# A GEGLU feed-forward kernel: two half loads of w_gate move from SyncE's DMA queue to ScalarE's

## The chip, the core and the metric

The kernel runs on one core of a Trainium2 chip. A core has TensorE (PE: matmuls, with the weight loads, PEld, beside them), VectorE (DVE), ScalarE (ACT), GpSimd (POOL) and SyncE (SP). Sixteen DMA engines move data between the chip's memory (HBM) and the core's on-chip memory (SBUF). A DMA is started by an instruction in the stream of some engine; in this kernel only SP and ACT do so. In the trace, `SPq` and `ACTq` mark those issuing instructions, and `q1` and `q10` are the two hardware queues that SP's and ACT's transfers travel on. Each engine works through its own instruction stream in order, so an issue that takes long holds up what stands behind it in that stream.

The metric is device time in microseconds (us) of one execution. The kernel before takes 276.43 us (median of 3 runs, 276.41 to 276.88).

## The reference

```python
def reference(x, w_gate, w_up, w_down):
    return (_gelu(x @ w_gate) * (x @ w_up)) @ w_down
```

`x` is 32 x 32 x 1024, that is 1024 rows of D = 1024; `w_gate` and `w_up` are 1024 x 3584 (F = 3584), `w_down` is 3584 x 1024. All are bf16; `_gelu` is the tanh approximation.

## The kernel before, in words

Stage 1 computes, for each of the 28 blocks of 128 columns of F, the gate and the up product against both halves of the rows (512 each), applies Gelu, multiplies, and keeps the result in `gT`. It saves matmuls with a seven-product scheme of the Strassen kind on 2 x 2 blocks: the inner dimension is split in two halves of KH = 4 tiles of 128, the weights' blocks are `a11`, `a12` (gate, first and second half of D) and `a21`, `a22` (up), and the blocks of x are `B11`, `B21` (first 512 rows, in the tile `xt0`) and `B12`, `B22` (last 512 rows, in `xt1`). Stage 2 multiplies `gT` by `w_down`, again with seven products.

A w_gate tile (`WG[c]`, line 86 loads it) holds two blocks of F; its first half in D serves `first_products` (a11 x B11), its second half `second_products` (a12 x B21). So `WG[1]` serves blocks 2 and 3, and `WG[4]` blocks 8 and 9. x comes in by three transposing DMAs on SP: B11 (line 131), B21 (line 149), and xt1 (line 155), which is twice as large.

The order of the work is written out by hand, and the streams keep it. At the start:

- PE runs ten warming matmuls (line 137), then `first_products` for blocks 0 to 7, `second_products` for blocks 0 to 7, first 8 and 9, second 8 and 9, first 10 (which needs `WG[5]`'s first half), and then the products on sums of x: T1 x S1, first 11, and T2 x S2.
- ACT issues six loads (WG0 in three pieces, the first halves of WG1, WG2 and WG3) between the warming matmuls, then copies each first product out of PSUM into `E1` (line 213), turns each second product into Gelu (line 220), seeds two accumulators `X` (line 226) after the Gelus of blocks 5 and 6, and copies the first products of blocks 8 and 9. A block's second product accumulates onto its first product in the same PSUM bank, so `second_products(n)` starts only when ACT's copy of block n is done.
- SP issues B11, then, after a small ACT write into B21 (line 147) that holds it back, B21, then the second halves of WG1 and WG2, half of the first w_up tile (line 93), the second half of WG3, the whole of WG4, xt1, both halves of WG5, and the other half of the w_up tile.
- DVE makes the sums of weights for blocks 0 and 1 and then the sums T1 to T4 of x, for which it needs xt1.

Of the kernel before, what the change touches and what calls it, by code (L numbers as in the profile page):

```python
# [12 lines left out]
def kernel(  # L13
# [18 lines left out]
    nc = tc.nc  # L32
# [10 lines left out]
    DT = D // P  # L43
    KH = DT // 2
# [38 lines left out]
    def load_gate(c, queue, lo=0, hi=DT):  # L83
        if c not in WG:
            WG[c] = gw.tile([P, DT, 2 * P], bf16, name="gw", tag="gw")
        queue.dma_start(  # L86
            out=WG[c][:, lo:hi, :], in_=wg_r[:, lo:hi, 2 * c * P : (2 * c + 2) * P]
        )

    def load_up(c, lo=0, hi=4):  # L90
        if c not in WU:
            WU[c] = uw.tile([P, DT, 4 * P], bf16, name="uw", tag="uw")
        nc.sync.dma_start(  # L93
            out=WU[c][:, :, lo * P : hi * P],
            in_=wu_r[:, :, (4 * c + lo) * P : (4 * c + hi) * P],
        )
# [4 lines left out]
    def a11(i):  # L101
        return block(WG, 2, i, 0)

    def a12(i):
        return block(WG, 2, i, 1)
# [18 lines left out]
    def psum_p(name):  # L124
        return psum.tile([P, NB], fp32, name=name, tag="p")

    def psum_q(name):
        return psum.tile([P, NB], fp32, name=name, tag="q")

    with tc.manual_schedule():  # L130
# [16 lines left out]
                nc.scalar.activation(B21[:, 0, 0:8], table, ACT.Copy)  # L147
                nc.scalar.activation(table, ones[:, 0:8], ACT.Gelu_apprx_tanh)
        nc.sync.dma_start_transpose(out=B21, in_=xf[0:NB, KH * P : D])
        for c in (1, 2):  # L150
            load_gate(c, nc.sync, KH, DT)
        load_up(0, 0, 2)
        load_gate(3, nc.sync, KH, DT)
        load_gate(4, nc.sync)
        nc.sync.dma_start_transpose(out=xt1, in_=xf[NB:N, :])  # L155
        load_gate(5, nc.sync, 0, KH)
        load_gate(5, nc.sync, KH, DT)
# [6 lines left out]
        def t_sum(name, a, b, step=2):  # L164
            for k in range(0, KH, step):
                ks = slice(k, k + step)
                nc.vector.tensor_tensor(T[name][:, ks, :], a[:, ks, :], b[:, ks, :], ALU.subtract)
# [24 lines left out]
        def pair_product(ps, lhs, rhs, first, cuts):  # L192
            for lo, hi in zip(cuts, cuts[1:]):
                for p, l in zip(ps, lhs):
                    for k in range(lo, hi):
                        nc.tensor.matmul(  # L196
                            p,
                            lhsT=l[:, k, :],
                            rhs=rhs[:, k, :],
                            start=(first and k == 0),  # L200
                            stop=(k == KH - 1),
                            skip_group_check=True,
                        )

        def first_products(*blocks, cuts=(0, KH)):
            for i in blocks:
                A[i] = psum_p("a") if 4 <= i < 8 else psum_q("a")
            pair_product([A[i] for i in blocks], [a11(i) for i in blocks], B11, True, cuts)
            for i in blocks:
                if i % 2 == 0:  # L210
                    pool, tag = (xpool, "e1") if i == LEAD - 2 else (ring, "ring")
                    E1[i // 2] = pool.tile([P, 2, NB], fp32, name="e1", tag=tag)
                nc.scalar.activation(E1[i // 2][:, i % 2, :], A[i], ACT.Copy)  # L213

        def second_products(*blocks, cuts=(0, KH)):
            pair_product([A[i] for i in blocks], [a12(i) for i in blocks], B21, False, cuts)
            for i in blocks:
                if i % 2 == 0:
                    GL[i // 2] = half.tile([P, 2, NB], bf16, name="gl0", tag="half")
                nc.scalar.activation(GL[i // 2][:, i % 2, :], A[i], ACT.Gelu_apprx_tanh)  # L220
# [3 lines left out]
        def seed(i):  # L224
            X[i] = psum_p("x")
            nc.scalar.activation(X[i], E1[i // 2][:, i % 2, :], ACT.Copy)
# [51 lines left out]
        t_sum("T3", B22, B12)  # L278
        t_sum("T4", B21, T["T2"])
        first_products(0, 1, cuts=(0, 2, KH))  # L280
        for n in range(2, 8):
            first_products(n)
        for n in range(8):
            second_products(n)
            if n in (5, 6):
                seed(n - 5)
        first_products(8)
# [34 lines left out]
        for i in range(2, FT + 1):  # L322
# [24 lines left out]
            if here and i % 2 == 0:  # L347
                c = i // 2 + (6 if i < 8 else 4)
# [194 lines left out]
```

## Time and profile before

| what | value |
|---|---|
| median of 3 runs | 276.43 us (276.41 to 276.88) |
| the profiled execution's own time | 276.04 us |
| its span, first to last instruction | 274.2 us |
| PE busy | 269.2 us, 98% of the span |
| ACT busy | 139.6 us, 51% |
| DVE busy | 189.2 us, 69% |
| POOL busy | 87.1 us, 32% |
| granted PE clock | 1.000 |
| read from HBM | 22.02 MB |

The span leaves out 1.8 us of the profiled execution that lie around it, and the profiled execution is 0.39 us below the median. An issue's row (`SPq`, `ACTq`) gives the time the issuing engine spent on the instruction, not the transfer; the time to landing is listed apart, per group. "Waits" rows tell how long an engine stood idle before an instruction and what released it. The chain of waits follows the work that ended last backwards from the end; printed in order of time it shows what set the time of each stretch.

### The profile page before, as it was taken

The numbers are of one execution on the slowest core, as the hardware profiler recorded it, in microseconds if no ns is written. First come the engines' busy times: TensorE is split into PE (matmuls) and PEld (weight loads), VectorE is DVE, ScalarE is ACT, GpSimd is POOL, SyncE is SP. The second block draws the span as 40 slices with busy tenths as digits, with TensorE's granted clock in tenths as the row PEclk, the third lists the DMA queues.
The fourth block names the chain that finished last, engine by engine and source line by source line (L and its number), as shares of the span: only waits on it lengthen the run. The fifth ranks groups of instructions, "written<-read, shape, count | busy, mean of one in ns | idle before, by whom it ended". The sixth has DMA issues, their size and how long they took to land.

```text
span 274.2 us, 3352 instructions
## 1 busy us (share of the span) xinstructions
PE 269.2 (98%) x1186; PEld 189.5 (69%) x1186; DVE 189.2 (69%) x226; ACT 139.6 (51%) x240; POOL 87.1 (32%) x81
## 2 busy tenths in 40 slices
PE   8998999999999999999999999999999999999995
PEld 2444677768777687776877768764447888888883
DVE  0068985866668666686666766759994999999800
ACT  4787765566556665566665666531100072770311
POOL 0000075845558455584455844600000000000000
PEclk9999999999999999999999999999999999999999
DMA  7999402153400034216370202359702000000221
GB/s 190 271 257 272 160 1 76 44 188 101 129 2 0 0 95 138 76 36 195 91 217 0 76 2 77 112 189 318 226 0 77 2 0 0 1 2 0 97 96 38
DMA packets 41024, 26.42 MB, mean 96 GB/s; under 512 B 9264, under 2 KB 41008, under 8 KB 41008
## 3 DMA queue, kind: packets, MB, share of 16 engines
q1 hardware_dynamic: 38208, 24.78, 30.7%
q10 hardware_dynamic: 2800, 1.44, 2.1%
q8 instruction: 9, 0.15, 0.2%
q14 instruction: 7, 0.06, 0.1%
HBM read 22.02 MB, written 2.10 MB: 88 GB/s over the span
## 4 chain that ended last, share of the span: by engine, by line
PE 91%; SPq 4%; DMA 3%; ACT 1%; issue 0%
PE x L196 19%; PE x L398 18%; PE y L115 18%; PE a L196 13%; PE x L115 9%; PE y L398 9%; PE z L398 4%; SPq L155 3%; DMA gw<-in_w_gate_dram 1%; DMA gT<-in_w_gate_dram 1%; SPq L86 1%; PE y L196 1%; ACT L139 0%; ACT e L213 0%; ACT o_sb L510 0%; SPq L93 0%
## 5 line engine op out<-in xcount | busy, mean ns | idle before, releaser
L196 PE MATMUL x<-T,s 128*128 128x512 f32 x224 | 63.4, 407 | 0.0
L196 PEld LDWEIGHTS x<-T,s 128*128 128x128 f32 x224 | 41.7, 188 | 10.9 <-ACT e L243 0.3
L196 PE MATMUL a<-xt,gw 128*128 128x512 bf16 x192 | 44.6, 380 | 0.2 <-DMA gw<-in_w_gate_dram 0.2
L185 POOL TENSOR_TENSOR s<-gw,s 128x512 fp32r<-128x512 bf16 x22 | 26.0, 1181 | 47.7 <-PE y L115 47.0
L260 DVE TENSOR_TENSOR u<-y,e 128x512 bf16<-128x512 f32 x28 | 19.3, 691 | 31.3 <-ACT e L258 30.5
L181 DVE TENSOR_TENSOR s<-s,gw 128x512 fp32r<-128x512 f32 x24 | 34.9, 1454 | 0.0
L196 PEld LDWEIGHTS <-gw 128*128 128x128 bf16 x192 | 17.4, 98 | 24.0 <-issue 4.4
L267 ACT ACTIVATE gl<-h 128x512 bf16<-128x512 bf16 x28 | 17.7, 631 | 27.6 <-DVE h L265 27.6
L247 DVE TENSOR_TENSOR gT<-gl,x 128x512 bf16<-128x512 bf16 x28 | 19.2, 687 | 17.9 <-PE x L115 17.9
L115 PE MATMUL x<-T,c 128*128 128x512 f32 x112 | 30.3, 392 | 0.0
L115 PE MATMUL y<-B,s 128*128 128x512 f32 x112 | 30.2, 391 | 0.0
L176 POOL TENSOR_TENSOR s<-uw 128x512 fp32r<-128x512 bf16 x25 | 29.1, 1166 | 0.0
L115 PE MATMUL y<-T,s 128*128 128x512 f32 x104 | 27.8, 389 | 0.0
L398 PE MATMUL x<-tc,sc 128*128 128x512 f32 x112 | 25.7, 389 | 0.0
L258 ACT ACTIVATE e<-x 128x512 f32<-128x512 f32 x28 | 16.7, 599 | 15.9 <-PE x L196 15.9
L213 ACT ACTIVATE e<-a 128x512 f32<-128x512 f32 x28 | 16.6, 596 | 16.0 <-PE a L196 15.9
L177 POOL TENSOR_TENSOR s<-gw,uw 128x512 fp32r<-128x512 bf16 x21 | 24.4, 1162 | 0.0
L115 PEld LDWEIGHTS y<-B,s 128*128 128x128 f32 x112 | 21.0, 188 | 4.8
L115 PEld LDWEIGHTS x<-T,c 128*128 128x128 f32 x112 | 20.9, 188 | 4.8 <-ACT e L258 0.5
L398 PEld LDWEIGHTS x<-tc,sc 128*128 128x128 f32 x112 | 21.0, 188 | 4.4
L115 PEld LDWEIGHTS y<-T,s 128*128 128x128 f32 x104 | 19.5, 188 | 4.0
L220 ACT ACTIVATE gl<-a 128x512 bf16<-128x512 f32 x28 | 16.7, 596 | 6.7 <-PE a L196 6.6
(58 smaller groups left out, 342.6 us busy)
## 6 DMA issues: line engine op xcount, KB each, us to landing
uw<-in_w_up_dram SPq DMA_DIRECT2D x6, 1024.0 KB, 6.4
gw<-in_w_gate_dram SPq DMA_DIRECT2D x8, 512.0 KB, 3.9
v<-in_w_down_dram SPq DMA_DIRECT2D x5, 512.0 KB, 3.6
v<-in_w_down_dram SPq DMA_DIRECT2D x4, 640.0 KB, 8.5
v<-in_w_down_dram SPq DMA_DIRECT2D x8, 256.0 KB, 4.4
out_dram<-o_sb SPq DMA_DIRECT2D x15, 128.0 KB, 1.7
gw<-in_w_gate_dram ACTq DMA_DIRECT2D x4, 256.0 KB, 4.4
uw<-in_w_up_dram SPq DMA_DIRECT2D x2, 512.0 KB, 6.2
```

Of the source, the lines that this page charges most:

```text
L115: nc.tensor.matmul(ps, lhsT=lhs[:, k, :], rhs=rhs[:, k, :], start=(first and k == 0), stop=(k == KH - 1), skip_group_check=True,)
L176: engine.tensor_tensor(S1[i], a21(i), a22(i), ALU.add)
L177: engine.tensor_tensor(S3[i], a11(i), a21(i), ALU.subtract)
L181: nc.vector.tensor_tensor(S2[i], S1[i], a11(i), ALU.subtract)
L185: engine.tensor_tensor(S4[i], a12(i), S2[i], ALU.subtract)
L196: nc.tensor.matmul(p, lhsT=l[:, k, :], rhs=rhs[:, k, :], start=(first and k == 0), stop=(k == KH - 1), skip_group_check=True,)
L220: nc.scalar.activation(GL[i // 2][:, i % 2, :], A[i], ACT.Gelu_apprx_tanh)
L247: nc.vector.tensor_tensor(gT[:, i, 0:NB], GL[i // 2][:, i % 2, :], X[i], ALU.mult)
L258: nc.scalar.activation(e3, X[i], ACT.Copy)
L260: nc.vector.tensor_tensor(U1[i], Y[i], e3, ALU.add)
L267: nc.scalar.activation(G1[i], h1, ACT.Gelu_apprx_tanh)
L398: nc.tensor.matmul(ps, lhsT=lhs[:, i, t * P : (t + 1) * P], rhs=rhs[:, i, :], start=(first and j == 0 and i == 0), stop=(last and j == JF ...
```

## The change

Two loads of 256 KB each leave SP's stream and enter ACT's. WG1's second half is now issued by ACT after the copies of the first products of blocks 0 and 1, and WG4's second half by ACT after the Gelu of block 1. SP keeps WG4's first half. Each load writes the same place from the same source as before. Nothing else moves: the order of the other instructions on PE, DVE, POOL, ACT and SP is the same.

```diff
-        for c in (1, 2):
-            load_gate(c, nc.sync, KH, DT)
+        load_gate(2, nc.sync, KH, DT)
         load_up(0, 0, 2)
         load_gate(3, nc.sync, KH, DT)
-        load_gate(4, nc.sync)
+        load_gate(4, nc.sync, 0, KH)
         nc.sync.dma_start_transpose(out=xt1, in_=xf[NB:N, :])
...
         first_products(0, 1, cuts=(0, 2, KH))
+        load_gate(1, nc.scalar, KH, DT)
         for n in range(2, 8):
             first_products(n)
         for n in range(8):
             second_products(n)
+            if n == 1:
+                load_gate(4, nc.scalar, KH, DT)
             if n in (5, 6):
                 seed(n - 5)
```

## The prediction

> **What bounds the kernel now.** I read the page first: the span is 274.2 us, and PE is busy for 269.2 us of it. A change of load order can only win back idle time of PE, or add some. So I asked for PE's rows in order of time. After its first product at 5.40 us there is one gap in the whole first stage, 0.83 us before the first product of block 10, ended by a load of w_gate (into gT's space: WG5's first half). The chain of waits, in order of time, says what made that load late:
>
> ```profile
> 12.42 7.83 SPq L155
> 20.25 0.04 issue
> 20.30 3.36 DMA gT<-in_w_gate_dram
> 23.66 0.05 issue
> 23.71 1.04 PE a L196 x4
> ```
>
> Columns: start, length, what. SP's issue of the transpose of xt1 takes 7.83 us; only then can WG5's first half be issued, and it lands 3.36 us later. From 23.71 on the chain is PE all the way to the last copy and store. So what moves the product at 23.71 moves the end by as much, and the most to be won is 0.83 us (plus nothing elsewhere).
>
> Next the issues of both queues, from the trace in order of time (start, length, engine):
>
> ```profile
> 0.74 1.42 SPq L131 DMA_TRANSPOSE xt<-in_x_dram  x1
> 1.83 0.43 ACTq L86 DMA_DIRECT2D gw<-in_w_gate_dram  x1
> 5.67 3.45 SPq L149 DMA_TRANSPOSE xt<-in_x_dram  x1
> 9.17 1.12 SPq L86 DMA_DIRECT2D gw<-in_w_gate_dram  x2
> 11.51 0.87 SPq L86 DMA_DIRECT2D gT<-in_w_gate_dram  x1
> 12.42 7.83 SPq L155 DMA_TRANSPOSE xt<-in_x_dram  x1
> ```
>
> B11 and B21 are equally large, yet B21's issue took 3.45 us and B11's 1.42. What differs is that ACT's loads were still under way. The transfers between 4.4 and 8.5 us:
>
> ```profile
> DMA packets 2407, 1.19 MB, mean 291 GB/s; under 512 B 80, under 2 KB 2407, under 8 KB 2407
> q10 hardware_dynamic: 2407, 1.19, 117.9%
> ```
>
> B21 was issued at 5.67, but up to 8.5 only ACT's queue q10 moved data. Between 8.5 and 10.5 us q1 moved 2019 packets, nearly all B21, and its issue ended at 9.12. So the two queues are not independent here: a transpose's issue stays open, and holds its engine, until the other queue's work has drained. xt1's 7.83 us is the same thing: it waits behind 1.75 MB of loads.
>
> Last, ACT's rows around the second new issue, since ACT executes that issue itself:
>
> ```profile
> 14.28 0.60 ACT L220 ACTIVATE gl<-a 128x512 bf16<-128x512 f32 x1 [0.27 <-PE a L196]
> 15.14 0.60 ACT L220 ACTIVATE gl<-a 128x512 bf16<-128x512 f32 x1 [0.27 <-PE a L196]
> ...
> 17.73 0.60 ACT L220 ACTIVATE gl<-a 128x512 bf16<-128x512 f32 x1 [0.27 <-PE a L196]
> 18.23 0.60 ACT L226 ACTIVATE x<-e 128x512 f32<-128x512 f32 x1
> 18.75 0.59 ACT L220 ACTIVATE gl<-a 128x512 bf16<-128x512 f32 x1
> 19.22 0.60 ACT L226 ACTIVATE x<-e 128x512 f32<-128x512 f32 x1
> 19.74 0.60 ACT L220 ACTIVATE gl<-a 128x512 bf16<-128x512 f32 x1
> 20.32 0.60 ACT L213 ACTIVATE e<-a 128x512 f32<-128x512 f32 x1
> ```
>
> The Gelu of block 1 runs 14.28 to 14.88. PE paces ACT with 0.27 us to spare per block, and back to back ACT starts an operation each 0.50 us (18.23 to 19.74, three steps). At 14.88, SP is in the middle of xt1's issue.
>
> **The change, part by part.** SP loses WG1's second half (1.12 / 2 = 0.56 us and a gap of 0.05) and half of WG4's issue (0.87 to about 0.56, so 0.31). xt1's issue opens 0.9 us earlier, at 11.5. That alone frees nothing, since the issue waits for data: between 10.5 and 18.4 us seven quarter-MB loads went ahead of xt1's bulk, 1.13 us each. WG1's half still goes ahead of it (it is issued at 8.2), WG4's second half does not. So xt1's bulk starts at about 17.3 instead of 18.4, and its issue ends at 20.25 - 1.13 = 19.1.
>
> WG1's second half on ACT: after the copy of block 1, at about 8.2 us, inside B21's issue (5.67 to 9.12). Cost on ACT 0.43 to 0.63 us by its six loads before, or up to 9.12 + 0.53 = 9.65 if it is held until SP's issue ends. ACT's copy of block 2 would start at 9.65 instead of 8.24; at 0.50 each against a pace of 0.86, ACT has caught up by block 6. The first waiter is PE's second product of block 0 at 12.33, which needs only copy 0. The tile itself is needed at 14.06 (block 2: 5.40 + 10 x 0.866) and lands about 3.5 us after its issue. I take 0 for it; without that cover it would cost 1.4 us at most, the delay of ACT.
>
> WG4's second half on ACT, at 14.88: its lower bound is ACT's own issue rows, 0.36 (the store at the end) to 0.63 us, which ACT's 0.27 us per block absorb in two blocks: cost 0. Its upper bound is that ACT is held until xt1's issue ends, 19.1, plus 0.1 to 0.53 of its own. The nearest row is B21's issue, which was held for 2.0 us longer than B11's while the other queue drained; the only load issued inside a transpose's issue, ACT's at 1.83, ended at 2.26, 0.10 after the transpose's issue ended at 2.16. Both fit being held, so I take the upper bound: ACT goes on at 19.4 (19.2 to 19.65).
>
> What stands behind it on ACT: the Gelus of blocks 2 to 5, a seed, Gelu 6, a seed, Gelu 7, and then the copy of block 8: eight operations of 0.50, then 0.60, so the copy ends at 19.4 + 4.6 = 24.0. PE's second product of block 8, at 21.0 before, waits for that copy. Second 8 and 9 take 1.73, and the first product of block 10 starts at 24.0 + 1.73 = 25.75 in place of 23.71: +2.05 us. WG5's stall is gone inside it: xt1 ends at about 20.6, WG4's second half follows and lands by 22.4, WG5's first half by 23.2, all before they are needed. DVE's sums of x start earlier than before (xt1 lands at about 21.1 instead of 22.3) and don't matter. After that ACT has no backlog that PE meets: from copy 8's end it is paced by second 8 and 9. POOL has nothing before 35 us and shifts with the rest; SP's later loads are released by buffers and shift too.
>
> Sum: 276.04 + 2.05 = 278.1 for an execution like the profiled one; with its 0.39 to the median, 278.5 us. The hold's ends give +1.5 to +2.6 (start of xt1's bulk 0.4 either way): 277.9 to 279.0.
>
> A rule of the Trainium skill bears on this: its page "Perfetto Trace Analysis", section "DMA Instruction — HWDGE (DVE, Sync)", says that the block which generates descriptors is shared by the two issuing engines and locked for one instruction until all its descriptors are made, and that the recorded issue includes the wait for that lock. By it ACT is held to the end of xt1's issue, the 278.5 above; without it, the 275.8 of the first rival. The early load that ended 0.10 us after B11's issue agrees, but that load met only 0.33 us of it.
>
> **The rivals.** (1) No hold, and the stall goes: 0.25. ACT's issue takes 0.5 us, and WG1's half, queued by 9 us behind B21, fills the slow start of the loads at 10.5 (the rate stays under about 110 GB/s for 0.5 us, against 290 otherwise, some 0.4 us lost); with six loads instead of seven ahead of xt1 the slow stretch before its bulk (17 to 18.5 us, mean 107 GB/s) shrinks by a seventh, 0.2. WG5's half lands 0.6 earlier, between 0.4 and the whole 0.83: 275.8 us (275.6 to 276.0). For it: ACT's five loads at 2.3 to 5.1 were taken in 0.5 us each with up to a MB outstanding. Against: B21's 3.45 us.
>
> (2) No hold, no gain: 0.13. What must be in SBUF before block 10 is the same number of bytes, and the 16 DMA engines are busy almost all of 2 to 24 us; WG4's half goes in among xt1's packets and xt1 ends when it did. 276.4 us (276.1 to 276.7). The Trainium skill has this as a rule ("DMA: Bandwidth & Descriptors", section "Issuing engines are not separate DMA queues": all run on the same engines and interleave). The trace shows the sharing, but between 4.4 and 8.5 us no interleaving.
>
> (3) Held in part: 0.15. ACT's issue gets through when xt1's packets begin to flow, at 16.4 to 18. Break-even is 23.71 - 1.73 - 4.6 = 17.3: a hold of 2.4 us. At 17.8 it is +0.5: 276.9 us.
>
> (4) ACT is not held but WG4's half travels behind all of xt1 and lands after 21.98, so that second 8 waits instead of first 10: 0.05, +0.3 to +0.7, 276.9.
>
> **How the numbers follow.** The held case has 0.42. About 0.2% (0.55 us) is what a measurement can tell from no change. Slower: 0.42, half of (3), all of (4): 0.55. Same: (2), half of (3), and a little of (1): 0.22. Faster: most of (1): 0.23. The range reaches from the low end of (1), 275.6, to the top of the held case, 279.0, and leaves out about 1 in 10; the held case by itself is 277.9 to 279.0.
>
> **What would show it.** Held: ACT's issue row at about 14.9 is 3 to 5 us long and ends with SP's issue of xt1; ACT's Gelus run back to back from 19.4; PE's only gap is before the second product of block 8, some 3 us, released by ACT's copy, and the gap at block 10 is gone. xt1's issue opens at 11.5 and ends near 19.1. I am wrong if ACT's second issue takes about 0.5 us: then PE's gap before block 10 tells (1) from (2), and a gap before the second product of block 8 released by the load is (4).

## The result

The changed kernel takes 275.66 us (median of 9 runs, 275.46 to 275.88) against 276.41 us before: a ratio of 0.9978, 95% interval 0.9968 to 0.9988. It is faster by about 0.2%, 0.75 us. The forecast was 278.5 us and slower; 275.66 lies near the low end of the range given, and next to the first rival's 275.8.

The chain of waits of the changed kernel, in order of time (start, length, what), now runs on PE from its first product on. SP's issue of xt1 and the load of WG5 no longer stand in it:

```profile
1.83 3.92 DMA gw<-in_w_gate_dram
5.75 0.05 issue
5.79 8.96 PE a L195 x39
14.75 0.05 issue
14.80 9.66 PE a L195 x44
24.46 1.85 PE y L195 x8
```

The issues of both engines in the changed kernel (start, length, engine):

```profile
5.92 3.64 SPq L149 DMA_TRANSPOSE xt<-in_x_dram  x1
...
12.13 6.16 SPq L154 DMA_TRANSPOSE xt<-in_x_dram  x1
18.34 1.13 SPq L86 DMA_DIRECT2D gT<-in_w_gate_dram  x2
...
8.10 0.37 ACTq L86 DMA_DIRECT2D gw<-in_w_gate_dram  x1
...
15.00 0.60 ACT L219 ACTIVATE gl<-a 128x512 bf16<-128x512 f32 x1 [0.27 <-PE a L195]
15.01 0.37 ACTq L86 DMA_DIRECT2D gT<-in_w_gate_dram  x1
15.86 0.60 ACT L219 ACTIVATE gl<-a 128x512 bf16<-128x512 f32 x1 [0.27 <-PE a L195]
```

ACT's second new issue stands in the middle of SP's issue of xt1 (12.13 to 18.29) and takes 0.37 us. It isn't held at all: the next Gelu waits for PE with the usual 0.27 us to spare. And xt1's issue is 6.16 us long instead of 7.83; WG5 is issued at 18.34 instead of 20.30.

Why it is shorter shows in the rate of the DMA engines from 10.3 to 18.7 us, in 40 slices of 0.21 us. First the kernel before:

```profile
GB/s 288 99 78 117 322 280 290 334 341 339 300 198 198 258 280 307 307 295 319 341 322 317 327 327 317 310 305 288 293 291 279 287 254 167 101 79 56 37 35 210
q1 hardware_dynamic: 4642, 2.08, 110.8%
```

The same stretch of the changed kernel:

```profile
GB/s 290 290 300 350 349 349 318 346 176 229 297 281 302 283 295 288 280 305 278 290 293 297 288 285 298 288 290 285 260 288 276 291 288 293 290 291 291 289 288 291
q1 hardware_dynamic: 6071, 2.19, 111.8%
q10 hardware_dynamic: 528, 0.26, 10.4%
```

Two holes of before are gone: the slow start after B21 (78 to 117 GB/s, three slices) and, above all, the slow stretch at the end (down to 35 GB/s, six slices). 2.45 MB (q1 and q10 together) moved in the 8.4 us instead of 2.08. In the slow stretch of before, 17 to 18.5 us, xt1's packets were under way already, mixed with the last ones of the loads:

```profile
DMA packets 492, 0.16 MB, mean 107 GB/s; under 512 B 352, under 2 KB 492, under 8 KB 492
q1 hardware_dynamic: 492, 0.16, 148.7%
```

The 352 packets under 512 B are xt1's, the other 140 are of the loads. Together they were open for 1.49 times the time that 16 engines have, and yet moved 107 GB/s. I read this as xt1's packets waiting, on DMA engines that were done with the loads, for others that were not; the trace doesn't tell the 16 engines apart, so that part is not shown.

To compare single executions I use one distance on PE: from the start of the first product of block 8 to the first product on T1. The rows of before, then of the changed kernel:

```profile
19.26 3.62 PE L196 MATMUL a<-xt,gT 128*128 128x512 bf16 x16
24.39 2.19 PE L196 MATMUL y<-T,s 128*128 128x512 f32 x8
19.98 4.48 PE L195 MATMUL a<-xt,gT 128*128 128x512 bf16 x20
24.11 2.20 PE L195 MATMUL y<-T,s 128*128 128x512 f32 x8
```

It is 24.39 - 19.26 = 5.13 us before and 24.11 - 19.98 = 4.13 us after. So the gap cost 1.00 us; the idle time listed for it, 0.83, counts from the modelled end of the matmul ahead. The profiled execution of the changed kernel (275.88 us) began its products 0.39 us later than the one before, at 5.79, and lost 0.33 more before block 8, so at the first product on T1 it is only 0.28 ahead, and its span is 0.1 shorter. That start lay between 5.26 and 5.79 us in all executions profiled with the loads of the start unchanged.

### The profile page after: what moved, and what is told of

Read it like the earlier page. It is cut to its first block, busy times and chain, and to the rows that moved or that the text cites. A ratio compares the mean times of both kernels' runs of the same rounds, so it can differ in the third digit from the quotient of the medians.

```text
span 274.1 us, 3340 instructions
## 1 busy us (share of the span) xinstructions
PE 268.7 (98%) x1172; PEld 189.7 (69%) x1186; DVE 189.2 (69%) x226; ACT 139.7 (51%) x240; POOL 87.2 (32%) x81
## 3 DMA queue, kind: packets, MB, share of 16 engines
q1 hardware_dynamic: 37168, 24.25, 30.4%
## 4 chain that ended last, share of the span: by engine, by line
PE 96%; DMA 1%; ACT 1%; issue 0%
PE x L195 19%; PE x L400 18%; PE y L115 18%; PE a L195 18%; PE y L400 9%; PE x L115 9%; PE z L400 4%; DMA gw<-in_w_gate_dram 1%; PE y L195 1%; ACT L139 0%; ACT o_sb L512 0%
## 5 line engine op out<-in xcount | busy, mean ns | idle before, releaser
L115 PEld LDWEIGHTS y<-T,s 128*128 128x128 f32 x104 | 19.5, 188 | 4.1
```

The lines of the kernel that those rows point to most:

```text
L115: nc.tensor.matmul(ps, lhsT=lhs[:, k, :], rhs=rhs[:, k, :], start=(first and k == 0), stop=(k == KH - 1), skip_group_check=True,)
```

## The experiments

Two theories were open once the trace was read. "Filled queue": WG1's half, queued on ACT's queue while B21 still moves, lets the loads start at once on all DMA engines and keeps these in step, so that xt1's transpose, taken to need all of them, starts without a wait. "Less ahead of xt1": what counts is WG4's half, which no longer stands ahead of xt1. Five rounds of runs each, unless said otherwise.

### Both kernels again

> The kernel before once more, for its profile. If the slow stretch of the DMA engines before xt1's bulk (17 to 18.5 us, 107 GB/s) and the slow start at 10.5 us belong to the kernel, both are there again, xt1's issue lasts 7 to 8 us and PE's gap before block 10 is 0.7 to 0.9 us. If the stretch was an accident of that one execution, it is shorter than 0.5 us and the gap is under 0.4 us.

> The changed kernel once more, as the yardstick of this group: 0.6 to 0.9 us faster than before. Theory 'filled queue': again no slow start at the end of B21 and no slow stretch before xt1, ACT's two issues 0.4 to 0.6 us each, no gap of PE before block 10. If the smooth stretch was an accident, the slow stretch is back here and the gap too.

The kernel before again (one execution, 276.14 us): slow start and slow stretch are back, xt1's issue takes 7.26 us, the distance on PE is 24.50 - 19.37 = 5.13 us. From 10.3 to 18.7 us:

```profile
GB/s 293 289 81 73 117 278 251 234 329 337 351 332 249 232 244 266 297 346 341 319 319 280 268 285 285 329 317 300 312 295 308 291 296 269 241 176 110 110 290 290
```

The changed kernel again: 0.9973 (0.9961 to 0.9985), 275.44 us against 276.27; issues of 0.37 and 0.38 us on ACT, xt1's issue 6.16 us, distance 23.61 - 19.48 = 4.13 us, no hole. Both patterns belong to their kernels.

### WG1's half alone, and WG4's half alone

```diff
-        for c in (1, 2):
-            load_gate(c, nc.sync, KH, DT)
+        load_gate(2, nc.sync, KH, DT)
...
         first_products(0, 1, cuts=(0, 2, KH))
+        load_gate(1, nc.scalar, KH, DT)
```

> WG1's second half alone goes over ACT's queue; WG4 is whole on SP. Theory 'filled queue' (the load queued on ACT's queue while B21 still moves lets the loads start at once and in step on all DMA engines): no slow start at 10.5, no slow stretch, xt1's bulk starts at 17.0 to 17.4, its issue ends near 19.2, PE has no gap before block 10: 0.6 to 0.8 us faster, as the whole change. Theory 'less ahead of xt1' (what counts is the quarter MB of WG4 that no longer stands before xt1): gap still 0.6 to 0.9, 0.0 to 0.2 us faster.

```diff
-        load_gate(4, nc.sync)
+        load_gate(4, nc.sync, 0, KH)
...
             second_products(n)
+            if n == 1:
+                load_gate(4, nc.scalar, KH, DT)
```

> WG4's second half alone goes over ACT's queue; WG1 stays on SP. Theory 'filled queue': slow start at 10.5 and a slow stretch before xt1 remain; xt1's bulk starts near 17.3, is mixed with WG4's half, and WG5's half lands at about the old time: 0.0 to 0.3 us faster. Theory 'less ahead of xt1': 0.6 to 0.8 us faster, as the whole change. The theory of the prediction (ACT held by xt1's issue) would make it 1.5 us or more slower; ACT's issue row tells: 0.4 us or 3 to 5.

WG1's half alone gives the whole gain: 0.9969 (0.9957 to 0.9980), 275.45 us, distance 23.51 - 19.38 = 4.13 us. xt1's issue ends at 18.81. The amount of data ahead of xt1 is the same as before, so the 1.2 to 1.4 us by which it ends earlier (20.25 and 19.97 before) are what the two holes cost. Its rate from 10.3 to 18.7 us:

```profile
GB/s 291 340 349 346 323 346 288 176 290 278 302 285 293 295 288 285 295 285 298 285 288 295 278 307 280 297 285 297 283 290 275 271 289 288 290 290 290 291 291 290
```

The moved load has a price too, ahead of the distance measured here. B21, whose transfer it follows, lands 6.7 us after its issue, at 12.4 us; before, it landed after 5.4, at 11.1. PE's second product of block 0 needs B21 and was due at 12.2 (5.26 + 32 matmuls of 0.217), so it had to wait, and ACT's Gelu behind it shows by how much:

```profile
xt<-in_x_dram SPq DMA_TRANSPOSE x1, 6.7
13.54 0.60 ACT L219 ACTIVATE gl<-a 128x512 bf16<-128x512 f32 x1 [0.57 <-PE a L195]
```

ACT waited 0.57 us instead of the usual 0.27, so 0.30 of the 1.00 us is given back. In the changed kernel it is 0.16 in the second execution (0.43 instead of 0.27) and nothing in the first, in which PE started later. Why B21 lands later with a load of the other queue behind it, these runs do not show.

WG4's half alone makes it slower: 1.0053 (1.0032 to 1.0073), 277.53 us, which neither theory had expected. From 16 to 20 us, slices of 0.1 us:

```profile
GB/s 266 230 271 220 220 292 333 297 282 277 279 261 271 272 243 282 246 187 166 143 110 85 41 46 38 38 41 36 102 136 128 133 123 120 115 161 289 289 287 289
```

The slow stretch is now longer, to 19.6 us. SP has less data ahead of xt1, but ACT's load went ahead of it all the same: from 14.8 to 19.6 us q10 moved all its 0.26 MB. xt1's issue takes 8.26 us, and PE's rows show the gap:

```profile
19.82 3.62 PE L196 MATMUL a<-xt,gT 128*128 128x512 bf16 x16
24.76 1.04 PE L196 MATMUL a<-xt,gT 128*128 128x512 bf16 x4 [1.33 <-DMA gT<-in_w_gate_dram]
```

1.33 us instead of 0.83, and the distance is 5.63 us, 0.50 more than before. That is less than the 1.26 us between the medians; the runs spread from 276.46 to 279.27, and the rest of the loss is not shown by this one execution (277.18), in which the first product started at 5.71. The slow start at 10.7 us is there as before. That the DMA engines were out of step when the extra load came in, and that its packets were taken up by those ahead and held back those behind, is my reading; it is not shown. ACT's issue took 0.37 us here too, at 14.84 inside SP's issue (12.74 to 21.00). So the loss is not the one that the prediction's theory had forecast here, 1.5 us or more by a held ACT.

### The same load, queued too late

```diff
         for n in range(2, 8):
             first_products(n)
+            if n == 3:
+                load_gate(1, nc.scalar, KH, DT)
```

(in place of the issue after blocks 0 and 1)

> As WG1 alone over ACT's queue, but ACT issues it two blocks later, after the copy of block 3 (9.5 to 10 us), when it can no longer be queued by the time B21 ends at 10.5. Theory 'filled queue': slow start at 10.5 and slow stretch before xt1 are back, xt1's issue ends at 19.8 to 20.6, PE's gap before block 10 is 0.6 to 1.4 us: between 0.2 us faster and 0.6 us slower than before. Rival 'the other queue as such' (SP has one issue less, or two queues move more): gap gone, 0.6 to 0.8 us faster, as WG1 alone. If WG1's half lands after 14.1 us there is a gap before the second product of block 2 too.

0.9991 (0.9972 to 1.0010): not to be told from before, though most runs lie at 275.6 to 276.1, and one at 278.62. From 10.3 to 18.7 us:

```profile
GB/s 293 289 291 271 166 54 173 236 346 344 341 349 344 339 351 280 302 283 297 293 288 295 285 297 283 285 295 290 293 290 295 283 302 272 273 276 191 140 291 290
```

The slow start is back (54 GB/s), and a stretch before xt1 too, but only two slices of it (191, 140). xt1's issue ends at 19.80, within what I expected, but the distance on PE is 23.95 - 19.73 = 4.22 us, so the gap is nearly gone in this execution, against what I expected. The landing of WG5's first half tells more: 23.2 us here (issued at 19.84, 3.4 to landing), 23.7 and 23.8 before, 22.1 with WG1's half in time. So the late load won about 0.5 of some 1.6 us. The gap is small all the same because PE reached block 8 at 19.73, 0.4 to 0.5 us later than in the two executions of before. Being late gives up most of the earlier landing. Why 0.5 us are left after a slow start as deep as before is open: here two queues had loads waiting, not one, and SP's batch ahead of xt1 was one load shorter.

### WG2's half instead of WG1's

```diff
-        for c in (1, 2):
-            load_gate(c, nc.sync, KH, DT)
+        load_gate(1, nc.sync, KH, DT)
...
         first_products(0, 1, cuts=(0, 2, KH))
+        load_gate(2, nc.scalar, KH, DT)
```

> WG2's second half goes over ACT's queue in the place of WG1's, at the same point; WG1 stays on SP. Theory 'filled queue': any load of that size queued there does it: no slow start, no slow stretch, no gap before block 10, 0.6 to 0.9 us faster, as WG1 alone. Rival 'WG1's order' (what counts is which load SP starts with): a slow stretch of 0.5 us or more, at most 0.4 us faster.

0.9974 (0.9964 to 0.9983), distance 23.79 - 19.66 = 4.13 us, no holes. Which of the two loads it is doesn't matter.

### A load that nobody needs

```diff
         first_products(0, 1, cuts=(0, 2, KH))
+        nc.scalar.dma_start(
+            out=gT[:, 0, :].rearrange("p (b f) -> p b f", f=2 * P),
+            in_=wg_r[:, 0:KH, 26 * P : 28 * P],
+        )
```

> The kernel before, nothing moved, with one more load of 256 KB on ACT's queue after the copy of block 1, of data that nobody uses, into a part of gT that is written over later. Theory 'filled queue': the load fills the time in which SP's loads start slowly, all DMA engines stay in step, the slow stretch before xt1 goes; the extra 0.9 us of data costs less than the 1.6 us won, xt1's bulk starts at 17.5 to 17.9, gap before block 10 0.1 to 0.5: 0.2 to 0.6 us faster although more is read. Rival 'less ahead of xt1': one load more ahead of xt1, gap 1.4 to 1.8: 0.6 to 0.9 us slower.

> The kernel with the unused 256 KB again, for its profile: whether its slow stretch (18.25 to 19.0 us) belongs to it. If so, xt1's bulk starts at 18.6 to 19.2 after a stretch of 0.4 us or more; if the stretch comes and goes, the bulk starts by 18.2 in one step and the gap before block 10 is under 0.6 us.

With 512 KB, the target is `gT[:, 0:2, :]` and the source all eight tiles of D:

> The kernel before with an unused load of 512 KB instead of 256 KB on ACT's queue after the copy of block 1. Theory 'filled queue, long enough' (SP's first load is issued at 9.2 to 9.6 and needs about 2.2 us until all DMA engines have its packets; the 256 KB were used up at about 11.6, just before): ACT's queue now covers to about 12.4, all engines stay in step, no slow stretch, xt1's bulk starts at 18.8 to 19.2, where the 256 KB had it, so the second 256 KB cost next to nothing: 0.2 us faster to 0.3 us slower than before. Rival 'bytes': 0.9 us more ahead of xt1 than with 256 KB, bulk at 19.7 to 20.0, gap before block 10 near 2 us: 0.8 to 1.2 us slower than before.

The 256 KB cost nothing and win nothing: 1.0002 (0.9994 to 1.0011), 276.51 us. That is neither of the two forecasts. The slow start at 10.5 us was filled, but SP's queue took over at 11.6 us with a dip, and a slow stretch remained. From 10.3 to 18.7 us:

```profile
GB/s 290 293 306 351 349 349 289 224 178 254 322 312 312 310 310 276 266 261 276 285 315 295 302 295 293 307 285 293 288 290 297 285 293 288 295 285 267 285 271 62
```

A second execution (276.73 us) has the stretch too, at 18.3 to 18.8, so it belongs to the kernel. The distances on PE are 5.38 and 5.44 us.

The 512 KB are the test of why. SP's first load was issued at 9.57 with the 256 KB. A load that SP issues onto idle DMA engines moves its first packets about 1 us later and reaches the full rate after about 2.2 us (issued at 29.50 in the kernel before; the full rate came at 31.75). The 256 KB were used up at about 11.7, just before that. The 512 KB last to 12.4:

```profile
GB/s 284 293 336 351 346 344 346 329 288 276 301 295 107 283 281 298 297 283 293 288 290 300 283 293 283 300 285 286 295 290 293 290 293 288 285 295 288 293 290 293
q1 hardware_dynamic: 4166, 1.94, 98.1%
q10 hardware_dynamic: 1040, 0.52, 22.2%
```

One single dip, no slow stretch, and xt1's bulk starts at 18.9 us, when it did with 256 KB less (18.75 to 19.0). The missing stretch was worth the 0.9 us that the second 256 KB take at 290 GB/s.

The hand-over alone does not explain the stretch with 256 KB, though. In the changed kernel SP's first load was issued at 9.61, so that its full rate was due at 11.8 us as well, and the rate dips as much at the hand-over (176 and 229 GB/s at 12 us), yet no stretch follows. What differs is that SP's batch is one load shorter there. So a filled start together with the shorter batch removes the stretch, and so does a filled start of 512 KB with the full batch; what each is worth by itself these runs do not separate.

The time with 512 KB is longer, 1.0028 (1.0017 to 1.0039), 277.13 us. Its 0.80 us over before is what the rival "bytes" had forecast, but the bulk's start and the gap of 0.47 us are not, and the loss has another place, a wait that I had not reckoned with:

```profile
13.62 7.07 PE L196 MATMUL a<-xt,gw 128*128 128x512 bf16 x32 [0.61 <-DMA xt<-in_x_dram]
20.52 3.62 PE L196 MATMUL a<-xt,gT 128*128 128x512 bf16 x16
24.61 1.04 PE L196 MATMUL a<-xt,gT 128*128 128x512 bf16 x4 [0.47 <-DMA gT<-in_w_gate_dram]
```

PE waits 0.61 us before 13.62, which is the second product of block 0 (32 matmuls, the first products of eight blocks, stand ahead of it). The row names xt, and B21 is indeed late. Its row, by time to landing:

```profile
xt<-in_x_dram SPq DMA_TRANSPOSE x1, 7.8
```

Issued at 5.67, it landed at 13.5, against 11.1 before. It is the wait that WG1's half alone showed with 0.30 us, longer with the longer load on ACT's queue.

### B21 in two transposes (three rounds)

```diff
-        nc.sync.dma_start_transpose(out=B21, in_=xf[0:NB, KH * P : D])
+        for lo in range(0, KH, 2):
+            nc.sync.dma_start_transpose(
+                out=B21[:, lo : lo + 2, :], in_=xf[0:NB, (KH + lo) * P : (KH + lo + 2) * P]
+            )
```

> The kernel before with B21's transpose in two transposes of half the size, one behind the other on SP. The prediction's reading (a transpose's issue is held until the other queue's work has drained, at 8.5): the first piece's issue, at 5.7, lasts 2.8 us or more. Rival 'own queue' (an issue stays open only while too many of SP's own transposing packets are outstanding; B11's 128 per engine fitted, and B21's did not quite): the first piece's issue lasts 0.7 to 0.9 us, and the second stays open to about 9. Time: within 0.4 us of before by both.

0.9997 (0.9986 to 1.0008). SP's rows:

```profile
5.68 1.23 SPq L150 DMA_TRANSPOSE xt<-in_x_dram  x1
...
6.96 2.50 SPq L150 DMA_TRANSPOSE xt<-in_x_dram  x1
```

The first half's issue ended at 6.91, 1.6 us before ACT's loads had drained at 8.5; only the second stayed open to 9.46. So an issue is not held by the other queue's work as such. That SP's own packets outstanding are the limit fits, though 1.23 us is more than the 0.7 to 0.9 I gave it.

### Earlier first loads, on top of WG1's half

```diff
+        load_gate(0, nc.scalar, 0, 2)
+        load_gate(0, nc.scalar, 2, KH)
         for n in range(NWARM):
...
-                load_gate(0, nc.scalar, 0, 2)
-                load_gate(0, nc.scalar, 2, KH)
```

> WG1 alone over ACT's queue, and besides ACT issues the first two pieces of WG0 before anything else, at about 0.75 us instead of 1.83. With the gap before block 10 gone, PE's only idle time is before its first product (5.26 to 5.8 us in the traces, the warming matmuls end at 5.2). If the pieces travel ahead of B11 and all lands by 5.2: first product at 5.2 to 5.3, 0.1 to 0.5 us faster than WG1 alone, 0.9 to 1.3 faster than before. If they delay B11 by their 0.45 us each: first product at 5.5 to 6.0, 0 to 0.5 us slower than WG1 alone.

1.0010 (0.9990 to 1.0031), 276.68 us, runs from 275.33 to 277.94. The gap before block 10 stays gone (24.25 - 20.12 = 4.13), but the first product now waits for B11:

```profile
6.31 13.97 PE L195 MATMUL a<-xt,gw 128*128 128x512 bf16 x63 [1.44 <-DMA xt<-in_x_dram]
```

It starts at 6.31 instead of 5.26, worse than the worst I gave. No version was faster than the changed kernel; WG1's half alone equals it.

## Why the prediction was wrong

**What bounds the kernel** was right: one gap before block 10, ended by WG5's half behind xt1, then PE to the end. The most to be won was put at 0.83 us; by the distance on PE it is 1.00.

**The step that failed is the reading of B21's 3.45 us**: that a transpose's issue "holds its engine until the other queue's work has drained", and from it that ACT, issuing inside xt1's issue, would be held until 19.1. The first half was a false cause (the split transpose shows it), and the second inferred from SP's wait that ACT would wait the other way. ACT's issue inside SP's transpose of xt1 took 0.37 or 0.38 us in all three executions that have WG4's half there. And xt1's 7.83 us were not "the same thing" as B21's 3.45: from 10.3 to 18.7 us of the kernel before only q1 moved data, so what xt1 waited behind were SP's own loads. The +2.05 us of the sum were therefore 0. The lower bound of that term, 0.36 to 0.63 us absorbed in ACT's slack, was in the text and was the true one; the nearest row for an ACT issue was an ACT issue, not SP's. The load at 1.83 that "ended 0.10 after" B11's issue could not bear the weight: it met that issue for 0.33 us, less than an issue takes anyway.

The rule of the Trainium skill that I leaned on ("Perfetto Trace Analysis", section "DMA Instruction — HWDGE (DVE, Sync)": the descriptor generator is locked for one instruction until all its descriptors are made), read as keeping ACT out for as long as SP's issue is open, does not describe these runs: SP's transpose was open for 6.16 us, and ACT's copy went through in its midst in 0.37. The measurement decides.

**WG1's half was costed at 0** because nothing waited for it. ACT's side of that was right. What was missed is that it carries the whole gain, 0.82 us in the group where it was measured alone, and WG4's half none: alone that one costs 1.26 us. It was missed too that B21 lands later with this load behind it, which cost PE up to 0.30 us.

**xt1's bulk** was put at 17.3 us, by one load less ahead of it. It started at about 16.25, since the holes closed as well: in the first rival I had let the slow stretch shrink by a seventh, and it went altogether. The issue opened at 12.13 (11.84 in the second trace), not 11.5, mostly because B21's issue ended later, at 9.56 and 9.27 instead of 9.12, and because the half of WG4 that SP kept took 0.69 us to issue, not 0.56.

**The rivals.** The first, "no hold, and the stall goes", is what happened: 275.8 us forecast, 275.66 measured, with the reason half right (the filled slow start) and at a chance of 0.25. That the number fits so well is partly luck: WG5's half landed 1.4 us earlier (22.2 instead of 23.7), not 0.6, and only the size of the gap kept the gain to 1.00 us. The second, that the same bytes on the same engines give no gain, falls: the bytes were the same with WG1's half alone, and it was 0.3% faster. The Trainium skill's rule behind it ("DMA: Bandwidth & Descriptors", section "Issuing engines are not separate DMA queues") says that transfers of all issuing engines run on the same DMA engines and interleave. The changed kernel's trace agrees: from 19.5 to 20.5 us q10 moved 405 packets and q1 463. The second queue was still worth 0.8 us here, by having packets ready when the first ran dry. The third and fourth need a held ACT or a late WG4, and neither was seen, but the fourth was near: WG4's half landed 6.3 us after its issue, at 21.3, and the second product of block 8 needed it at 21.7; in the second trace 0.2 us were to spare.

## What to carry to other kernels

Before a row of one engine is taken as the price of another engine's instruction, look for the same kind of instruction on the same engine: ACT's own issues were the better row. Where a large transpose follows a batch of loads, look at the rate slice by slice: in these traces a batch that started slowly, on DMA engines run dry, ended in a slow stretch, and the wait showed only there. A load that is due anyway, queued on the second queue early enough to cover the first one's start-up, repaired that; another load, queued at 14.84 us behind a slow start, made it worse. Look also at what the earlier queued load holds up: here B21 landed later.

## What was not expected of the hardware

- A small hole costs again later. The slow start of before (about 0.6 us at some 100 GB/s) was followed by a slow stretch of over 1 us ahead of xt1, 6 us later. A load of 256 KB moved to the other queue, ahead of the hole, removed both with equal data (xt1's issue ended at 18.81 instead of 19.97 to 20.25). That the one hole causes the other is argued from these pairs, not seen in the trace.
- 256 KB of useless data can cost the transfer behind them nothing: with 512 instead of 256 KB, xt1's bulk started at 18.9 us all the same, without a slow stretch. The kernel paid elsewhere, in a later landing of B21 (13.5 us).
- A load of 256 KB issued on the other queue at 14.84 us, behind a slow start, made xt1 wait longer with the same data ahead of it (xt1's issue took 8.26 us instead of 7.26 to 7.83).
- A load queued on ACT's queue while B21's transpose was open delayed B21's landing: from 11.1 us to 12.4 with 256 KB and 13.5 with 512 KB.
